# At most three of the first 26 bulk loads outstanding at a time, in an attention and rational-MLP kernel on one core

## The chip, the cores and the metric

The kernel runs on one NeuronCore of a Trainium2 chip. The metric is the device time of one execution in microseconds. Before the change three runs gave a median of 906.75 us (906.69 to 906.97).

## The reference, cut to what matters

```python
# q, k, v: (8 batches, 8 heads, 576 positions, 64)
scores = np.matmul(q, k.transpose(0, 1, 3, 2)) / sqrt(64)
# heads 0-3 see the last 32 positions; heads 4-7 every fourth of the last 128
scores = np.where(masks, scores, -1e9)
attn = exp(scores - max); attn = attn / (attn.sum(-1) + 1e-09)
x = (attn @ v)                          # as 4608 tokens x 512
h = x @ w_in                            # 512 -> 2048
P = a0 + a1*h + a2*h**2 + a3*h**3
Q = 1 + |b0|*|h| + |b1|*h**2
out = (P / (Q + 1e-6)) @ w_out          # 2048 -> 512
```

All inputs of the attention are float32; the two weight matrices come as 64-bit floats.

## The kernel before, in words

**Work.** The attention is cut into 48 units, six per batch. A unit loads one block of queries and keys (`load_qk`, 448 KB) and one of values (`load_v`, 384 KB). TensorE makes 48 small matmuls of scores, VectorE takes maxima and differences, ScalarE the exponentials, VectorE the sums and reciprocals, GpSimd the normalisation. In batch 0 TensorE then transposes the probabilities (three matmuls, `transposes`), somebody copies them out of the PSUM, and 48 more matmuls with the values (`av`) follow; VectorE transposes the result into place (`turn_out`). The MLP runs in tiles of 512 tokens x 128 hidden features, 144 of them: h matmuls, a rational function in about a dozen VectorE, ScalarE and GpSimd instructions, and out matmuls. All large matmuls split their operands into a high and a low part, except the first eight tiles, which use plain float32.

**Weights.** The 16 blocks of w_in and the 16 of w_out are loaded once (`w_fetch`, 512 KB each, since they are 64 bits wide). Each is turned into float32 by a scale on ScalarE (L718, tile wi_f or wo_f), a conversion of the low word on ScalarE or GpSimd (L318 or L726, tile wi_raw or wo_raw) and a join on VectorE (L324, tile w), and then split (tiles wi and wo).

**Order.** A planner (`Plan.run`) decides once, at build time, the order of the instructions of every engine, and each engine's queue is fixed in that order (`pin`). All transfers are issued by SyncE (SP), one after the other, by `load`; an SP instruction that waits holds up all SP instructions behind it. The tile framework has eight landing semaphores that transfers take in turn, so that a transfer is issued no earlier than the landing of the eighth one ahead of it, whatever its kind.

**The first transfers.** SP issues the six coefficients and the mask and then, in this order, the loads that are counted below as load 1 to 26 (q for a block of queries and keys, v for values, i for w_in, o for w_out): q q v q v q v q v q v q v i q v v o i o i, here two small stores of leftover tokens (left), o i q, another such store, o q. More small stores, the moves of batch 1's probabilities through HBM (turned, pT) and the other weights follow. Loads 1 to 11 and 13 are those of batch 0; the first h tile of the MLP needs all six units of batch 0 and load 14.

The instructions of the program itself come to the engines by DMA too; the profile counts them apart from the kernel's queue q1, as queues q8 and q14.

Of the kernel before, what the change touches and what calls it, by code (L numbers as in the profile page):

```python
# [19 lines left out]
P = 128  # L20
# [21 lines left out]

DEPTH, LOADS, STAGE, AHEAD, ON_PE = 2, 2, 6, 6, 2
PE_TURNS = 1
LEFT = S - 512
RQ, RKEY, NV = 4 * 3 * 32, 4 * 128, 3 * 2 * 2 * 64
LOG_SHIFT = 40
# [122 lines left out]
class Plan:  # L170
# [12 lines left out]
    def op(self, engs, rank, fn, *deps, dma=0, lock=False):  # L183
        o = Op(engs, rank, fn, deps, dma, lock)
        self.ops.append(o)
        return o
# [100 lines left out]
def tile_attention_moe(  # L287
# [10 lines left out]
    nc = tc.nc  # L298
# [8 lines left out]
    pin = tc.keep_in_program_order  # L307
# [3 lines left out]
    def load(dst, src):  # L311
        pin(nc.sync.dma_start(dst, src))

    def mm(o, lhs, rhs, start=True, stop=True):
        pin(nc.tensor.matmul(o, lhs, rhs, start=start, stop=stop))  # L315

# [43 lines left out]
    class Unit:  # L360
        def __init__(self, b, u):
            self.b, self.u, self.n = b, u, b * NU + u
            self.start, self.on_pe, self.pe_turn = b == 0, b < ON_PE, b < PE_TURNS
            self.s_tag, self.o_tag = (START_S[u], START_O[u]) if self.start else ("att", "att")
            self.s, self.o_ps = two_banks(self.s_tag), two_banks(self.o_tag)

        def load_qk(self, pool, tag):
            t = pool.tile([P, RQ + RKEY], F32, tag=tag, name=f"qk{self.n}", bufs=LOADS if pool is att else 1)
            load(t, qk[self.n])
            self.q = t[:, :RQ].rearrange("p (g i c) -> p g i c", g=4, i=3)  # L370
            self.k = t[:, RQ:].rearrange("p (g k) -> p g k", g=4)

        def load_v(self, pool, tag):
            self.v = pool.tile([P, NV], F32, tag=tag, name=f"v{self.n}", bufs=LOADS if pool is att else 1)
            load(self.v, vp[self.n])

        def scores(self):
            on_pe = self.on_pe
            if on_pe:

                for j, cnt, m in self.masks():
                    for r in range(j // 3, (j + cnt) // 3):
                        mm(self.s[:, r, :192], ident_b, m[:, 3 * r - j : 3 * r - j + 3], start=True, stop=False)
            for i in range(3):
                for g in range(4):
                    for r in range(2):
                        half = slice(64 * r, 64 * r + 64)
                        mm(self.s[32 * g : 32 * g + 32, r, 64 * i : 64 * i + 64], self.q[half, g, i], self.k[half, g, 32 * i : 32 * i + 64], start=not on_pe, stop=not on_pe or i == 2)
# [98 lines left out]
        def av(self):  # L487
            v_t = self.v.rearrange("p (i h e d) -> p i h e d", i=3, h=2, e=2)
            for i in range(3):
                for g in range(4):  # L490
                    h, e = g // 2, g % 2
                    for r in range(2):
                        half = slice(64 * r, 64 * r + 64)
                        c0, c1 = 192 + 64 * i, P * i + 32 * g if self.pe_turn else 96 * g + 32 * i
                        mm(self.o_ps[32 * g : 32 * g + 32, r, c0 : c0 + 64], self.pT[half, c1 : c1 + 32], v_t[half, i, h, e])
# [12 lines left out]
        def pieces(self):  # L508
# [14 lines left out]
            for s0, t0, step, num in segs:  # L523
                n_main = max(0, min(num, -(-(512 - t0) // step)))
                if num > n_main:

                    t1 = t0 + step * n_main - 512
                    to = LEFT * self.b + (t1 if step == 1 else LEFT // 4 * (t1 % 4) + t1 // 4)
                    left.append(((s0 + n_main, num - n_main), (slice(None), kts, slice(to, to + num - n_main))))
# [99 lines left out]
        def finish(self, av):  # L629
# [38 lines left out]
            if left:  # L668
                lf = op({"SP": 430 * len(left)}, self.by + 20.0, lambda e: self.put_left(), to, dma=P * 2 * LEFT * 4 + 60000)
                lf.count = len(left)  # L670
# [35 lines left out]
    def w_fetch(key):  # L706
        kind, n = key
        raw[key] = r = wpool.tile([P, 512], w_in.dtype, tag="%s%d" % key, name="%s_raw%d" % key)
        load(r, w_in[n] if kind == "wi" else w_out[n * P : (n + 1) * P, :])

    def w_words(key):
        return raw[key].bitcast(I32).rearrange("p (n two) -> p n two", two=2)
# [40 lines left out]

    def plan_weights(key):
        f = op({"SP": 430}, 0, lambda e: w_fetch(key), dma=512 * (8 if wide else 4) * P)
        early.append(f)
        if len(joined) >= AHEAD:
# [305 lines left out]
    for kt in range(NK):  # L1063
        r = NF * (NC - 2) + 2.0 + 2 * kt
# [99 lines left out]
```

## Time and profile before

| | |
|---|---|
| median of three runs | 906.75 us |
| profiled execution | 904.86 us |
| its span, first to last instruction | 903.1 us |
| mean granted TensorE clock | 0.992 of 2.4 GHz |
| PE busy | 879.2 us, 97% of the span, 8042 matmuls |
| DVE, ACT, POOL busy | 721.2, 669.4, 476.1 us |
| DMA | 89.24 MB, mean 99 GB/s |
| PE's share of the chain that ended last | 85% |

PE is TensorE, PEld its weight loads, DVE VectorE, ACT ScalarE, POOL GpSimd, SPq the instructions by which SyncE issues transfers. The profiled execution is 1.76 us longer than its span; the runs shown have a median 1.89 us above the profiled execution. Times in the rows count from the span's start.

### The profile page before, as it was taken

What the parts mean: (1) busy time and instruction counts of PE and PEld (TensorE: products, weight loads), DVE (VectorE), ACT (ScalarE), POOL (GpSimd) and SP (SyncE); (2) the same over time, 40 slices, a digit from 0 to 9 for tenths busy, and PEclk for the clock granted to TensorE, in tenths of its full rate; (3) what the DMA queues carried; (4) which work ended last, traced back from release to release, by engine and by line L of the source; (5) the groups of instructions that cost most, each with busy time, mean ns of one, the idle gap of its engine ahead of it and who ended that gap; (6) DMA issues with size and microseconds to landing.
All of it is one profiled execution on the core that took longest, in us unless ns stands there. A gap on an engine that the chain in (4) does not pass through costs nothing.

```text
span 903.1 us, 20437 instructions
## 1 busy us (share of the span) xinstructions
PE 879.2 (97%) x8042; PEld 689.5 (76%) x8042; DVE 721.2 (80%) x1301; ACT 669.4 (74%) x1070; POOL 476.1 (53%) x434
## 2 busy tenths in 40 slices
PE   5699999999999999999999999999999999999998
PEld 3344588888888888888888888888888888888886
DVE  4899999998998788887877888866986677656655
ACT  1977798877667778777777777777777777777766
POOL 1767366754545565654555555554555444444433
PEclk9899999999999999999999999999999999999999
DMA  9955851421523234332312335311420020001001
GB/s 342 318 181 156 296 184 42 141 76 67 180 84 107 65 109 160 112 94 68 131 48 77 90 114 153 92 35 32 143 58 18 1 82 0 1 1 48 1 0 47
DMA packets 70880, 89.24 MB, mean 99 GB/s; under 512 B 37376, under 2 KB 48256, under 8 KB 70784
## 3 DMA queue, kind: packets, MB, share of 16 engines
q1 hardware_dynamic: 70784, 87.94, 30.0%
q8 instruction: 63, 1.03, 0.5%
q14 instruction: 33, 0.27, 0.1%
HBM read 68.13 MB, written 19.79 MB: 97 GB/s over the span
## 4 chain that ended last, share of the span: by engine, by line
PE 85%; DVE 8%; ACT 2%; issue 2%; POOL 2%; DMA 0%; SPq 0%; DVEq 0%; POOLq 0%; ACTq 0%
PE out L315 40%; PE h L315 39%; PE pair L315 5%; DVE h L324 1%; DVE a L324 1%; DVE w L324 1%; ACT r L318 1%; DVE t L321 1%; DMA qk<-in_qk_dram 0%; POOL a L327 0%; DVE sm L442 0%; POOL p L327 0%; PE pair_A L315 0%; DVE wo L321 0%; DVE y L506 0%
## 5 line engine op out<-in xcount | busy, mean ns | idle before, releaser
L315 PE MATMUL h<-xh,wi 128*128 128x512 f32 x1072 | 356.7, 394 | 0.6 <-DVE a L324 0.6
L315 PE MATMUL out<-gh,wo 128*128 128x512 f32 x1072 | 332.1, 391 | 0.0
L327 POOL TENSOR_TENSOR a<-r,a 128x512 f32<-128x512 f32 x127 | 164.2, 1293 | 296.6 <-ACT r L318 285.3
L315 PEld LDWEIGHTS h<-xh,wi 128*128 128x128 f32 x1072 | 201.1, 188 | 48.4 <-DVE a L324 3.9
L315 PEld LDWEIGHTS out<-gh,wo 128*128 128x128 f32 x1072 | 200.0, 188 | 42.2
L315 PE MATMUL out<-gl,wo 128*128 128x512 f32 x536 | 209.0, 390 | 0.7 <-POOL gl L327 0.7
L315 PE MATMUL h<-xl,wi 128*128 128x512 f32 x536 | 208.8, 390 | 0.0
L324 DVE SCALAR_TENSOR_TENSOR a<-a,r 128x512 f32<-128x512 f32 x141 | 103.6, 735 | 105.6 <-ACT r L318 102.5
L327 POOL TENSOR_TENSOR gl<-a,gh 128x512 fp32r<-128x512 f32 x123 | 161.8, 1316 | 11.5 <-ACT gh L318 10.9
L318 ACT ACTIVATE r<-a,ln_bias 128x512 f32<-128x512 f32 x141 | 101.7, 721 | 89.1 <-POOL a L327 83.2
L318 ACT ACTIVATE t<-h,na_t 128x512 f32<-128x512 f32 x142 | 109.7, 772 | 28.9 <-PE h L315 28.3
L318 ACT ACTIVATE r<-a,ab_t 128x512 f32<-128x512 f32 x141 | 115.0, 816 | 20.9 <-DVE h L324 13.2
L324 DVE SCALAR_TENSOR_TENSOR h<-h,na_t,r 128x512 f32<-128x512 f32 x142 | 106.7, 751 | 14.4 <-ACT r L318 13.9
L315 PEld LDWEIGHTS out<-gl,wo 128*128 128x128 f32 x536 | 100.6, 188 | 22.8 <-POOL gl L327 1.8
L315 PEld LDWEIGHTS h<-xl,wi 128*128 128x128 f32 x536 | 100.7, 188 | 20.4 <-POOL xl L327 0.2
L324 DVE SCALAR_TENSOR_TENSOR h<-t,na_t,h 128x512 f32<-128x512 f32 x142 | 106.8, 752 | 4.1
L318 ACT ACTIVATE r<-r,exp_bias 128x512 f32<-128x512 f32 x144 | 104.0, 723 | 4.4
L321 DVE TENSOR_TENSOR t<-t,h 128x512 f32<-128x512 f32 x142 | 96.2, 678 | 9.8 <-ACT t L318 8.4
L318 ACT ACTIVATE a<-h 128x512 f32<-128x512 f32 x140 | 82.6, 590 | 27.1 <-PE h L315 26.6
L324 DVE SCALAR_TENSOR_TENSOR a<-a,h 128x512 f32<-128x512 f32 x132 | 90.3, 684 | 3.8
L318 ACT ACTIVATE gh<-a 128x512 fp32r<-128x512 f32 x122 | 75.9, 622 | 11.8 <-DVE a L324 9.6
L327 POOL TENSOR_TENSOR p<-p,sm 128x384 f32<-128x384 f32 x48 | 40.9, 855 | 36.1 <-DVE sm L446 28.3
(123 smaller groups left out, 771.9 us busy)
## 6 DMA issues: line engine op xcount, KB each, us to landing
qk<-in_qk_dram SPq DMA_DIRECT2D x48, 448.0 KB, 4.7
v<-in_vp_dram SPq DMA_DIRECT2D x48, 384.0 KB, 3.7
out_dram<-os SPq DMA_DIRECT2D x36, 256.0 KB, 2.3
wi_raw<-in_w_in_dram SPq DMA_DIRECT2D x16, 512.0 KB, 6.7
wo_raw<-in_w_out_dram SPq DMA_DIRECT2D x16, 512.0 KB, 6.4
turned<-u SPq DMA_DIRECT2D x42, 192.0 KB, 2.0
pT<-turned SPq DMA_DIRECT2D x84, 96.0 KB, 2.6
part<-os SPq DMA_DIRECT2D x4, 256.0 KB, 5.8
```

Source lines behind the costliest of these rows:

```text
L315: pin(nc.tensor.matmul(o, lhs, rhs, start=start, stop=stop))
L318: pin(nc.scalar.activation(o, i, func, **kw))
L321: pin(nc.vector.tensor_tensor(o, x, y, op))
L324: pin(nc.vector.scalar_tensor_tensor(o, x, s, y, op0, op1))
L327: pin(nc.gpsimd.tensor_tensor(o, x, y, op))
```

## The change: what it does

A second helper, `load_bulk`, does what `load` does, and counts its transfers in a list. For those with numbers 3 to 25 of the list (the fourth to the twenty-sixth) it adds a dependency on the transfer three places earlier in the list: SP waits until that one has landed. The blocks of queries and keys, of values and of weights are loaded by it; the coefficients, the mask, the stores and the moves through HBM still go by `load` and aren't counted. The order of all instructions on all engines is the same.

```diff
+BULK, GATED = 3, 26
...
+    bulk = []
+
+    def load_bulk(dst, src):
+
+        d = nc.sync.dma_start(dst, src)
+        pin(d)
+        if BULK <= len(bulk) < GATED:
+            tc.add_manual_dep(d.ins, bulk[-BULK].name, mybir.DependencyInfo(mybir.DependencyClass.Sync, mybir.DependencyReason.DATA), reason="few transfers at once")
+        bulk.append(d.ins)
+
...
-            load(t, qk[self.n])
+            load_bulk(t, qk[self.n])
...
-            load(self.v, vp[self.n])
+            load_bulk(self.v, vp[self.n])
...
-        load(r, w_in[n] if kind == "wi" else w_out[n * P : (n + 1) * P, :])
+        load_bulk(r, w_in[n] if kind == "wi" else w_out[n * P : (n + 1) * P, :])
```

## Rows read from the trace of the kernel before

**Rows 1.** The page: busy time of PE, and the span in 40 slices of 22.6 us (PE's busy tenths, the granted clock in tenths).

```profile
PE 879.2 (97%) x8042; PEld 689.5 (76%) x8042; DVE 721.2 (80%) x1301; ACT 669.4 (74%) x1070; POOL 476.1 (53%) x434
...
PE   5699999999999999999999999999999999999998
...
PEclk9899999999999999999999999999999999999999
```

**Rows 2.** Waits of PE in the first 60 us: who waited for whom, us in total, times, longest.

```profile
PE out L315 <- DVE g L324: 4.7, 1, 4.7
PE pair_B L315 <- issue: 3.2, 1, 3.2
```

**Rows 3.** The chain of waits in order of time, 16.5 to 28.5 us: start us, us, what.

```profile
16.57 3.18 issue
19.75 0.38 PE pair_B L315 x2
...
22.71 0.92 PE t L455 x3
...
25.64 1.13 PE pair_A L315 x48
...
27.45 0.98 DVE w L324
```

**Rows 4.** The timeline of DVE at the same place: start us, us, instruction, and in brackets the idle time before it and who ended that.

```profile
16.95 0.16 DVE L419 TENSOR_SCALAR mx<-mx 128x6 f32<-128x6 f32 x1
20.15 0.65 DVE L506 STREAM_TRANSPOSE x<-pair_B 128x192 f32<-128x192 f32 x2 [3.04 <-PE pair_B L315]
```

**Rows 5.** First the page's line for the queue q8 over the whole span, and the same queue from the start to 17.2 us, to 17.3 us and to 213.6 us (queue, kind: packets that have started, MB, share), and all packets of the stretch from 213.4 to 213.6 us; then the stretches from the start to 12.50, 17.27 and 213.51 us (start:end length, busy us and count in brackets of PE, PEld, DVE, ACT and POOL, granted clock, DMA share, GB/s).

```profile
q8 instruction: 63, 1.03, 0.5%
...
q8 instruction: 1, 0.02, 0.4%
...
q8 instruction: 2, 0.03, 0.8%
...
q8 instruction: 18, 0.29, 0.5%
...
DMA packets 1, 0.02 MB, mean 82 GB/s; under 512 B 0, under 2 KB 0, under 8 KB 0
...
0.00:12.50 12.50, 5.82 (x190) 3.94 (x192) 5.06 (x14) 2.53 (x4) 2.85 (x13) 1.00 0.82 286
...
0.00:17.27 17.27, 9.76 (x350) 6.93 (x351) 8.55 (x23) 4.07 (x7) 3.49 (x14) 1.00 0.87 320
...
0.00:213.51 213.51, 194.26 (x2246) 131.84 (x2247) 191.02 (x361) 159.47 (x270) 125.94 (x130) 0.97 0.55 189
```

**Rows 6.** SP's timeline: start us, us, transfer. These are loads 11, 14, 15, 19, 21, 22, 23, 24, 25 and 26, and the two small stores that come after load 26.

```profile
7.94 0.33 SPq L312 DMA_DIRECT2D v<-in_vp_dram  x1
...
11.38 0.33 SPq L312 DMA_DIRECT2D wi_raw<-in_w_in_dram  x1
13.49 0.33 SPq L312 DMA_DIRECT2D qk<-in_qk_dram  x1
...
17.70 0.33 SPq L312 DMA_DIRECT2D wi_raw<-in_w_in_dram  x1
...
19.74 0.33 SPq L312 DMA_DIRECT2D wi_raw<-in_w_in_dram  x1
...
27.90 1.17 SPq L312 DMA_DIRECT2D wo_raw<-in_w_out_dram  x1
29.12 0.42 SPq L312 DMA_DIRECT2D wi_raw<-in_w_in_dram  x1
29.64 0.38 SPq L312 DMA_DIRECT2D qk<-in_qk_dram  x1
...
30.66 0.49 SPq L312 DMA_DIRECT2D wo_raw<-in_w_out_dram  x1
31.97 0.33 SPq L312 DMA_DIRECT2D qk<-in_qk_dram  x1
...
34.26 1.03 SPq L312 DMA_DIRECT2D left<-y  x2
```

**Rows 7.** DMA issues of one transfer each (KB, us from issue to landing): load 1, issued at 1.65 us; load 19, issued at 17.70; a block of queries and keys issued at 82.4 us and one of values issued at 173.7 us, each with no other transfer ahead of it.

```profile
qk<-in_qk_dram SPq DMA_DIRECT2D x1, 448.0 KB, 4.0
...
wi_raw<-in_w_in_dram SPq DMA_DIRECT2D x1, 512.0 KB, 9.0
...
qk<-in_qk_dram SPq DMA_DIRECT2D x1, 448.0 KB, 3.5
...
v<-in_vp_dram SPq DMA_DIRECT2D x1, 384.0 KB, 2.9
```

**Rows 8.** The timeline of ACT where loads 18 and 19 are first read: start us, us, instruction.

```profile
28.12 0.73 ACT L318 ACTIVATE wo_raw<-wo_raw,low_bias 128x512 int32<-128x512 uint32 x1
...
29.32 0.74 ACT L318 ACTIVATE wi_raw<-wi_raw,low_bias 128x512 int32<-128x512 uint32 x1
```

**Rows 9.** Three stretches, with the columns of Rows 5: the one with the clock at half, the one after the longest wait of PE, and the rest of the span from 75 us on.

```profile
19.00:29.20 10.20, 7.48 (x226) 5.25 (x227) 7.52 (x21) 5.85 (x20) 3.68 (x5) 0.50 0.88 339
...
46.30:49.70 3.40, 3.40 (x6) 1.11 (x4) 3.40 (x4) 3.37 (x6) 1.66 (x2) 0.50 0.86 293
...
75.00:903.00 828.00, 822.49 (x7047) 659.33 (x7036) 662.64 (x1183) 621.21 (x980) 433.46 (x382) 1.00 0.26 83
```

## The prediction

> **What bounds the kernel now.** I read the page first, for where PE is idle, then PE's waits, the chain in order of time, and the timelines around the first transfers. PE is busy for 879 of 903 us and idle only in the first slices [rows 1]; from 75 us on it is busy 822.5 of 828 us [rows 9]. So a microsecond is won or lost in the start alone, and counts in full if the chain of the start is that much earlier where the dense stretch begins.
>
> Two waits of PE in the start are long. The 4.7 us for VectorE's g belong to the MLP's first tile. The other, 3.2 us, has no releaser: "issue", the engine waited for nothing that the profile shows [rows 2]. The chain passes through it: 3.18 us from 16.57 on, in the midst of a run of equal matmuls, and then VectorE, which has been idle for 3.04 us, goes on with the transpose of what these matmuls made [rows 3, 4]. After it the chain is PE, VectorE, ScalarE and GpSimd work.
>
> What PE waited for shows in the queue q8. Its 63 packets of 1.03 MB stand against PE's 16084 recorded instructions, 255 to a packet of 64-byte instructions: they are PE's program [rows 1, 5]. The second packet starts between 17.2 and 17.3 us, within the idle 3.18 us, when 701 instructions have started [rows 5]; PE goes on 2.48 us after 17.27. Far on, with no other transfer under way, the eighteenth packet starts when 4493 have started, 115 short of 18 x 256 [rows 5]. By the same measure the second was due at 512 - 115 = 397, and PE had begun 382 at 12.50 [rows 5], so it was due at about 12.6 us and came 4.7 us late. All that time the loads filled the DMA engines (share 0.82 up to 12.50 and 0.87 up to 17.27, at 286 and 320 GB/s, the empty first microseconds included) [rows 5]. I read it as an instruction packet that stood behind the loads' descriptors.
>
> The loads themselves: eight are outstanding at a time, since each issue waits for the landing of the eighth one ahead. Load 11 is issued at 7.94 when load 3 lands, load 21 at 19.74 when load 13 does. The ten steps between take 11.80 us, 1.18 each; one, 11.38 to 13.49, is 2.11, just after the first packet; without its extra 1.03 a load takes 1.08 us [rows 6].
>
> **The change part by part.** *The instruction packet.* From the due time of 12.6 to the stall at 16.57 lie 4.0 us, and a packet needs 2.48 from its start to PE: a delay of up to 1.5 us costs nothing, each microsecond more one of PE's. With three loads outstanding at most 3 x 1.08 = 3.2 us of loads can stand ahead: stall 1.7, so 3.04 - 1.7 = 1.3 us won on VectorE's wait [rows 4]. At the other end none stands ahead, and all 3.04 go. If the lateness has another cause, nothing goes. I take the middle of the queue, 1.6 us: 0.1 us of stall is left, and the chain is 2.9 us earlier.
>
> The Trainium skill says otherwise (DMA: Bandwidth & Descriptors, Queues, rings and completion order): each DMA engine goes round-robin between the queues for which it has work, a packet at a time. By that rule an instruction packet waits for a load's packet or so however many loads are queued, and the change would win nothing; that result is the first rival. The 4.7 us of delay speak against it, unless the packet was also asked for late.
>
> *The gates' own cost.* Each gated load is issued when the third one ahead has landed, so three loads take at least as long as one alone from issue to landing. Alone a block of values takes 2.9 us, one of queries and keys 3.5; load 1, in the cold start, took 4.0 [rows 7]. Three steps take 3 x 1.08 = 3.2 us. So the gates cost from nothing (2.9) over 0.1 us a load (3.5) to 0.26 a load (4.0); a gain is not excluded either, since the first loads then share the engines with fewer, but they land one after the other already, and I give it nothing. Nearest are the lone transfers. Only the queries' loads exceed 3.2, by 0.3; up to load 19 five triples end on such a load, but a late landing is partly made up by the next one, which has its data queued: I take a third of 5 x 0.3, 0.4 to 0.5 us later at load 19, with 0 and 16 x 0.26 = 4.2 us as ends.
>
> *What that delay meets.* Load 19 lands at 17.70 + 9.0 = 26.7 us [rows 6, 7] and ScalarE reads it at 29.32, after load 18 at 28.12 [rows 8]: 2.6 us of room. If the chain is 2.9 us earlier, ScalarE wants it at 26.4, and it lands at 27.1 or 27.2: ScalarE waits 0.7. ScalarE is close to full in that stretch and feeds the first h and out tiles, so I count it: 2.9 - 0.7 = 2.2 us won.
>
> *What is queued behind the gates on SP.* Up to load 21 nothing but loads. Load 22 was issued at 27.90, after stores that waited for VectorE, and now also waits for load 19 (26.7): no cost. Loads 23 and 24 wait for 20 and 21, which follow load 19 by some 1.25 us each (27.9 and 29.2); they were issued at 29.12 and 29.64: none. Load 25 waits for load 22, which alone takes 3.5 to 4.0 from 27.90, so 31.4 to 31.9 against 30.66, and load 26 for load 23, a step on, about 33 against 31.97 [rows 6, 7]. Behind it the next stores stood at 34.26 [rows 6]: a microsecond of room, cost nothing. If all work comes 2.2 us earlier, those stores want 32.1 and these gates cost SP a microsecond; the stores and load 27 are read much later, so I leave it at nothing. The other 22 loads and the moves are not gated, and the waits themselves are SP's, which is idle.
>
> *Sum.* -2.9 + 0.7 = -2.2 us. Against the profiled execution (span 903.1, 904.9 with what lies around it) that is 902.7; the runs' median is 1.9 above it, 906.75, and becomes 904.6. The likeliest case alone spans a gain of 1.2 to 3.0: 903.7 to 905.6.
>
> **The rivals.** *Nothing is won.* The packet is late for another reason, or three loads keep the engines as full as eight, and the stall stays. For it: 4.7 us of delay is some four loads and not eight, so the queue ahead of the packet may be bounded by something shorter than the outstanding loads, and three would come near that bound. Against it: three steps are still less than 4.7 us. Also in it: the dependency orders nothing that the queue didn't. Time 906.7, give or take 0.5.
>
> *Slower: the loads become the bound.* Load 19 has 29.32 - 26.7 = 2.6 us of room over the 16 loads since load 3, so from 2.6 / 16 = 0.16 us more per load (1.24, a triple of 3.7 us) ScalarE waits for weights, whether or not PE's stall is gone. At the 4.0 us of load 1 it is 0.26 per load, load 19 lands 4.2 us later and ScalarE waits 1.6: 908.4. For it: load 1's time, and that three outstanding leave no reserve if one of the 16 engines lags, as after the first packet (the step of 2.11). Against it: both lone transfers lie under 3.7.
>
> *More is won, by the clock.* The granted clock is 0.50, the 1.2 GHz level, from 19.0 to 29.2 us, after PE's idle 3.18; and again from 46.3, after the 4.7 [rows 2, 9]. Three pieces of the chain lie in the first stretch, 0.38 + 0.92 + 1.13 = 2.43 us [rows 3]. If PE stays busy and the clock stays up, half of that is won too: 904.6 - 1.2 = 903.4. Against it: PE is busy only 7.5 of those 10.2 us [rows 9] with waits for VectorE and GpSimd that stay.
>
> **How the numbers follow.** Forecast 0.46, nothing won 0.28, slower 0.15, clock 0.11. A measurement here tells 0.2% from no change, 1.8 us, so faster is below 904.9 and slower above 908.6 for my chances. Of the forecast's 0.46 some 0.38 lies below 904.9; with the clock and a little chance, faster 0.50. Slower: the case's time of 908.4 lies at the edge, and with delays up to several us more half to two thirds of it are beyond; with some unnamed mishap 0.14. The rest, 0.36, is the same. The range takes in the gain of the clock and most of the slower case: 903.0 to 907.8.
>
> **What would show it.** Right: in the profile after, PE's wait on "issue" near 16.6 us is gone or under 1 us, the second q8 packet starts before 16 us, VectorE's transpose starts near 17 us, and PE's dense stretch begins about 2 us earlier. The loads' issues follow each other by 1.1 us as before. Wrong: the packet still starts near 17 us (nothing won); or issues follow each other by 1.25 us or more, and ScalarE or PE waits for DMA of wi_raw, wo_raw or qk (slower). It would also be wrong if the start is shorter and the dense stretch begins when it did, because something in 30 to 75 us, such as the SP queue or the later weights, does not move with it.

## The result, and the profile after

The change makes the kernel slower: 912.4 us (median of 6 runs, 909.7 to 915.0) where the kernel before has 906.9 in the same comparison, a ratio of 1.0057 with an interval of 1.0033 to 1.0081. The forecast was 904.6 us and the range ended at 907.8. The profiled execution took 913.5 us, with a span of 911.7, 8.6 us more than the profiled one before; the medians lie 5.6 apart.

The page after, busy times, the 40 slices of PE, clock and DMA, and the chain by engine:

```profile
PE 882.0 (97%) x8042; PEld 691.0 (76%) x8042; DVE 720.6 (79%) x1301; ACT 669.6 (73%) x1070; POOL 475.7 (52%) x434
...
PE   5779999999999999999999999999999999999998
...
PEclk9699999999999999999999999999999999999999
DMA  7973771313433234331221334310521020001001
...
PE 84%; DMA 7%; DVE 6%; ACT 2%; issue 1%; POOL 1%; SPq 0%; POOLq 0%; ACTq 0%; DVEq 0%
```

PE's work is the same [rows 1]; its idle time and the clock's low stretches are in the first slices again. New is that 7% of the chain is DMA, where it was 0%. SP's timeline after, cut to loads 6, 7, 10, 12, 13, 16 with 17, and 21 (start us, us, transfer):

```profile
7.81 0.33 SPq L319 DMA_DIRECT2D qk<-in_qk_dram  x1
9.71 0.33 SPq L319 DMA_DIRECT2D v<-in_vp_dram  x1
...
14.10 0.33 SPq L319 DMA_DIRECT2D qk<-in_qk_dram  x1
...
16.86 0.33 SPq L319 DMA_DIRECT2D qk<-in_qk_dram  x1
20.00 0.33 SPq L319 DMA_DIRECT2D v<-in_vp_dram  x1
...
23.30 2.37 SPq L319 DMA_DIRECT2D v<-in_vp_dram  x2
...
31.50 0.33 SPq L319 DMA_DIRECT2D wi_raw<-in_w_in_dram  x1
```

A load is now issued when the third one ahead has landed, so load 3 landed at 7.8 us and load 13 at 23.3: ten steps of 1.55 us, where they were 1.18 [rows 6]. Load 21 is issued at 31.5 instead of 19.7 and lands at 36.3 instead of 29.2. Who waited, in the first 60 us: first PE, then ScalarE (ACT), then GpSimd (POOL) (us in total, times, longest).

```profile
PE h L326 <- ACT x L329: 4.6, 1, 4.6
...
PE pair L326 <- DMA pT<-turned: 2.0, 1, 2.0
PE pair_B L326 <- issue: 1.9, 1, 1.9
```

```profile
ACT wo_raw L329 <- DMA wo_raw<-in_w_out_dram: 4.6, 2, 3.6
```

```profile
POOL wo_raw L737 <- DMA wo_raw<-in_w_out_dram: 4.0, 1, 4.0
```

The wait on "issue" is there, at 1.9 us instead of 3.2 [rows 2]. But ScalarE and GpSimd now wait for weights: ScalarE reads load 18 at 31.51 instead of 28.12 us [rows 8].

```profile
31.51 0.76 ACT L329 ACTIVATE wo_raw<-wo_raw,low_bias 128x512 int32<-128x512 uint32 x1 [3.59 <-DMA wo_raw<-in_w_out_dram]
```

PE's second h tile waits 4.6 us for ScalarE behind them and starts at 38.49 instead of 35.31 us (PE's timeline, before and after):

```profile
35.31 5.64 PE L315 MATMUL h<-x,w 128*128 128x512 f32 x12 [0.94 <-ACT x L318]
```

```profile
38.49 8.27 PE L326 MATMUL h<-x,w 128*128 128x512 f32 x12 [4.57 <-ACT x L329]
```

The loss then grows, to 6.6 us at PE's matmul of 57.76 us (64.36 after). The chain shows a part of how (start us, us, what):

```profile
41.82 4.20 DMA turned<-u
46.02 0.02 issue
46.04 7.90 DMA pT<-turned
53.94 0.14 issue
54.08 2.37 PE pair L326 x97
```

Loads 27 to 30, which no gate holds, were issued at 42.3 to 45.2 us, just ahead of the moves of batch 1's probabilities. They were issued ahead of them before, too, at 35.84 to 39.95 us, but spread wider. A move that had taken 5.95 us took 7.9 behind them, and PE waited 2.0 us for it.

### The profile page after: what moved, and what is told of

Read it like the earlier page. It is cut to its first block, busy times and chain, and to the rows that moved or that the text cites. A ratio compares the mean times of both kernels' runs of the same rounds, so it can differ in the third digit from the quotient of the medians.

```text
span 911.7 us, 20435 instructions
## 1 busy us (share of the span) xinstructions
PE 882.0 (97%) x8042; PEld 691.0 (76%) x8042; DVE 720.6 (79%) x1301; ACT 669.6 (73%) x1070; POOL 475.7 (52%) x434
## 3 DMA queue, kind: packets, MB, share of 16 engines
q8 instruction: 63, 1.03, 0.5%
## 4 chain that ended last, share of the span: by engine, by line
PE 84%; DMA 7%; DVE 6%; ACT 2%; issue 1%; POOL 1%; SPq 0%; POOLq 0%; ACTq 0%; DVEq 0%
PE out L326 40%; PE h L326 39%; PE pair L326 5%; DMA qk<-in_qk_dram 2%; DMA v<-in_vp_dram 1%; DMA left<-y 1%; DVE h L335 1%; DMA pT<-turned 1%; DVE w L335 1%; DVE a L335 1%; DMA turned<-u 1%; DVE t L332 1%; DMA wi_raw<-in_w_in_dram 1%; DMA wo_raw<-in_w_out_dram 0%; ACT r L329 0%
## 5 line engine op out<-in xcount | busy, mean ns | idle before, releaser
L329 ACT ACTIVATE a<-h 128x512 f32<-128x512 f32 x140 | 82.6, 590 | 26.7 <-PE h L326 26.1
L329 ACT ACTIVATE gh<-a 128x512 fp32r<-128x512 f32 x122 | 75.9, 622 | 11.8 <-DVE a L335 9.7
L338 POOL TENSOR_TENSOR p<-p,sm 128x384 f32<-128x384 f32 x48 | 40.9, 854 | 35.4 <-DVE sm L457 30.9
```

Source lines behind the costliest of these rows:

```text
L329: pin(nc.scalar.activation(o, i, func, **kw))
L338: pin(nc.gpsimd.tensor_tensor(o, x, y, op))
```

## The experiments

In each, the kernel before ran beside on the same chip; ratios are against that. "Step" is the time between the landings of loads 3 and 13, divided by ten. Where a run stands below with a time alone, it was executed once.

**How many loads outstanding.** One number of the change is altered.

```diff
-BULK, GATED = 3, 26
+BULK, GATED = 4, 26      # e1; 5 in e2, 2 in e3, 1 in e13
```

Four:

> At most four loads outstanding instead of three. Theory A (queues run dry: a load takes some 4.7 us from issue to landing even with few ahead, so the step between landings is 4.7 us divided by the number outstanding): step 1.2 us instead of the change's 1.58, load 21 lands near 29 to 30 us instead of 36.3, time 906 to 908. Theory B (each gate costs its own half microsecond on SP whatever the depth): step 1.5 or more, load 21 near 35 us, time 911 to 912. Theory C (the loads' landings do not matter, the loss comes from the moves and stores that stand behind the gates on SP): time falls by a quarter of the loss at most, 910 to 912, since the gates are still there.

Five:

> At most five outstanding. Theory A: 4.7 / 5 = 0.94 us, below the 1.08 us that the engines need, so the step is that of before, load 21 lands near 29 us, and the second instruction packet still stands behind less than before: PE's idle on issue near 17 us falls under the 3.2 us of before; time 905 to 907, no slower than before. Theory B: still 910 to 912.

Two:

> At most two outstanding (the second load is not gated, the third to the twenty-sixth are). Theory A: 4 to 4.5 us divided by two, a step of 2.0 to 2.2 us, load 21 lands near 46 us, ten later than with three; time 919 to 924. Theory B: the same step as with three, 1.58 us, time 912 to 913. The second instruction packet: if it stands behind the loads, it starts before 15 us and PE's idle on issue is under 1 us.

One:

> One load outstanding at a time. The prediction took 3.2 us from issue to landing for a load alone (2.9 and 3.5 far on in the kernel). If that holds in the start too, the step is 3.0 to 3.5 us, load 13 lands near 5 + 12 x 3.2 = 43 us, and what failed is that two loads ahead add 1.4 us to it. If a load alone takes 4 us or more here (the cold start's 4.0), the step is 4 us or more and the lone transfers were the wrong rows.

| outstanding | step, us | step x number: issue to landing | GB/s, 12 to 24 us | second packet, us after PE's 397th instruction | PE's idle on issue near 17 us | ratio to before |
|---|---|---|---|---|---|---|
| 8 (before) | 1.18 | 9.4 | 410 | 4.7 | 3.18 | 1 |
| 5 | 1.13 | 5.6 | 377 | 3.1 | 1.26 | 0.9996 (0.9987 to 1.0006) |
| 4 | 1.34 | 5.4 | 326 | 2.0 | 1.54 | 0.9996 (0.9987 to 1.0006) |
| 3 (the change) | 1.55 | 4.7 | 257 | 2.3 | 1.88 | 1.0057 (1.0033 to 1.0081) |
| 2 | 1.89 | 3.8 | 231 | 2.1 | 0.19 | 1.0169 (1.0153 to 1.0185) |
| 1 | 3.16 | 3.2 | 143 | 2.1 | none | 951.6 us in one run beside 905.1 |

PE's 397th recorded instruction, weight loads counted, is where the prediction put the moment at which the second packet is due.

The stretch from 12 to 24 us in the kernel before, with five, four, three, two and one (length, busy us and count of PE, PEld, DVE, ACT, POOL, granted clock, DMA share, GB/s):

```profile
12.00:24.00 12.00, 8.26 (x288) 5.93 (x288) 7.35 (x21) 2.35 (x6) 1.73 (x3) 0.79 1.03 410
```

```profile
12.00:24.00 12.00, 8.01 (x347) 5.93 (x326) 8.98 (x28) 4.99 (x18) 2.57 (x4) 0.92 1.01 377
```

```profile
12.00:24.00 12.00, 7.57 (x350) 5.71 (x349) 9.49 (x29) 4.46 (x17) 2.90 (x5) 1.00 0.94 326
```

```profile
12.00:24.00 12.00, 8.34 (x302) 6.04 (x301) 8.01 (x22) 3.00 (x11) 1.77 (x3) 0.85 0.81 257
```

```profile
12.00:24.00 12.00, 8.01 (x257) 6.01 (x256) 6.69 (x19) 1.54 (x3) 1.66 (x3) 1.00 0.73 231
```

```profile
12.00:24.00 12.00, 4.89 (x154) 3.69 (x154) 3.64 (x10) 0.99 (x2) 1.06 (x2) 1.00 0.46 143
```

The DMA engines run dry: the two last columns fall with every load fewer. Theory B, a fixed cost per gate, falls with the row of four. Theory A has the sign right, and its constant of 4.7 us wrong: with four the step was to be 1.2 us and load 21 to land near 30, and they came at 1.34 and 32.6; with five load 21 lands at 31.2, 2 us later than before, at no cost in time. One load alone takes 3.2 us in the start too, as the lone rows said [rows 7]; what they didn't say is that each load outstanding beside it adds 0.6 to 0.9 us (3.2, 3.8, 4.7, 5.4), while the engines are busy for only 0.46, 0.73, 0.81 and 0.94 of the time. So three take 4.7 us, not 3.2.

The stall is a less steady quantity than one column suggests. A second trace with five outstanding (e11 below) has PE idle for 3.52 us and the packet 4.4 us after the 397th instruction, although up to load 14 its loads are those of e2; one with eight (e9) has 2.32 and 3.7, one with four (e10) 1.90 and 2.8, one with three up to load 13 (e4) 0.70 and 1.9. So the packet comes sooner with four and fewer (1.9 to 2.8 us) than with five and eight (3.1 to 4.7), but five and eight can't be told apart; with six halves of loads (e12 and e14 below) it came after 2.2 and 3.7. Some 2.1 us are left even with one load outstanding, so not all of the 4.7 us was the loads' doing. With two the packet starts at 17.41 us, not before 15, because PE itself waited for its loads.

With four, the first part of the forecast is there: PE's timeline (start us, us, instruction, idle before it and who ended it).

```profile
17.30 0.27 PE L326 MATMUL pair_B<-v,pT 64*32 64x64 f32 x2 [1.54 <-issue]
...
35.44 1.22 PE L326 MATMUL h<-x,w 128*128 128x512 f32 x1 [3.79 <-ACT x L329]
```

PE goes on at 17.30 instead of 19.75 [rows 3], and up to the first h tile all its work is 2.4 to 3 us earlier (29.66 against 32.39). The second h tile starts at 35.44 instead of 35.31: ScalarE had to wait for weights that landed 3.0 to 3.4 us later than before (load 21 at 32.6). What the instruction packet gave, the weights took.

**Which loads are gated.** With three outstanding, only the first part, and only the second:

```diff
-BULK, GATED = 3, 26
+BULK, GATED = 3, 13                                # e4
...
-        if BULK <= len(bulk) < GATED:
+        if 13 <= len(bulk) < GATED:                # e5
```

> Three outstanding for loads 4 to 13 only (the attention's first loads); loads 14 to 26 are free. Theory A: load 13 lands near 23 us as with the change, the weights then land 1.1 to 1.3 us apart, load 21 near 32 to 33 us instead of 36.3; ScalarE wants them from 29 us on: about half of the loss is left, time 908 to 910. Theory C (what stands behind the gates of loads 22 to 26 on SP makes the loss): time as before, 906.9. If the attention's own loads make the loss by PE's waits for them (0.3 to 1.2 us each): 910 to 912.

> Three outstanding for loads 14 to 26 only; loads 4 to 13 are free as before. Queues run dry: load 13 lands near 20 us as before, then steps of 1.5 to 1.6 us, load 21 near 32 to 33 us; PE's idle on issue near 16.6 us stays 2.5 to 3.2; ScalarE or GpSimd waits for the weights; with the late weights on top of the late PE the time is 908 to 911. If the loss came from the attention's loads alone, it is the time of before, within 0.2%.

Gates on loads 4 to 13 alone cost 0.20% (1.0010 to 1.0029 around 1.0020; load 13 lands at 23.3, load 21 at 33.1), on 14 to 26 alone 0.18% (1.0008 to 1.0028; load 13 at 20.0, load 21 at 32.7). The first is within what was expected, the second at its lower edge. Each costs some 1.7 us; together they cost 5. Load 21 is 3.9 and 3.5 us late in the two, and 7.1 late with both: the late landings add up, and the 2.6 us of room that the prediction found before ScalarE's read can be used only once. That last step is argued from the sums. That stores and moves behind the gates make the whole loss (theory C) does not hold: e4 has no gate after load 13 and pays.

**Only the first loads, five outstanding.**

```diff
-BULK, GATED = 3, 26
+BULK, GATED = 5, 13
```

> Five outstanding for loads 4 to 13, then free. If the instruction packet stands behind the loads and five are enough to keep the engines full: load 13 lands near 19.7 us, load 19 near 27, PE's idle on issue 1.3 us or less, the chain 2 us earlier at 20 us; the weights land when they did, so of the 2 us at most 1.5 are kept: 904.0 to 905.5 where the kernel before has 905.5. If the weights' landing (DMA throughput up to load 21) is the real bound of the first h tile: no gain, 905.3 to 906.

The landings are those of before (load 13 at 19.8, 19 at 26.7, 21 at 29.2), so here the gates cost the loads nothing, and still there is no gain: 1.0008 (0.9999 to 1.0016). Its PE timeline, and the same transposes in the kernel before:

```profile
18.41 0.27 PE L326 MATMUL pair_B<-v,pT 64*32 64x64 f32 x2 [2.97 <-issue]
...
30.17 0.87 PE L466 MATMUL t<-ident,p 128*128 128x128 f32 x3 [1.68 <-issue]
```

```profile
30.03 0.52 PE L455 MATMUL t<-ident,p 128*128 128x128 f32 x3 [0.25 <-PE pair_B L315]
```

PE reaches the first stall 1.1 us sooner and leaves it 1.3 us sooner (18.41 against 19.75); the stall itself, which was to be 1.3 us or less, stays at 2.97. Near 28.5 us it runs out of instructions again, for 1.68 us, and goes on at 30.17, where before it went on at 30.03. The fourth packet starts at 27.6 us in both kernels, when the freed loads 18 to 21 fill the queue. In the kernel before PE goes on with the same transposes 2.4 us after that packet starts, as after other packets; its gap there is only 0.25 us, and the profile names PE itself as the releaser, so that the packet would have been next there too is read from these times.

**Other orders.** If late weights eat the gain, weights issued earlier should keep it: loads 15 to 17, which batch 1 needs, are held until load 21 is issued, with no gates, with four and with five outstanding.

```diff
...
-            o.fn(eng)
+            if o.bulk:
+                seen += 1
+            if o.bulk and seen in (15, 16, 17):
+                held.append((o.fn, eng))
+            else:
+                o.fn(eng)
+            if o.bulk and seen == 21:
+                for fn, e in held:
+                    fn(e)
...
```

> No load gated, as before, but loads 15, 16 and 17 (batch 1) issued after loads 18 to 21 (weights): these weights land some 3 us earlier, near 23 to 26 us. If PE's late instruction packets and not the weights set the first h tile in the kernel before: no gain over before (905.0 to 906.0), PE's idle on issue near 17 us stays about 3 us. If the weights set it: 903 to 904.5.

> The same order, with at most four outstanding of the first 26. With four in the old order the chain was 3 us earlier at 21 us and lost that to weights that landed 2 to 3 us later. If those two are the whole story, the earlier weights keep most of it: first h tile near 30 us, the second near 33, time 903 to 904.5. If something else in the start takes the gain (the fourth instruction packet, the moves on SP): 905 to 906.

> The same order, with at most five outstanding. With five in the old order the fourth instruction packet came at 28.0 us and held PE to 30.5. If the packet stands behind five loads again: PE on issue near 29 us, time 905 to 906. If not: like four, 903 to 904.5.

None is faster: 1.0006 (0.9997 to 1.0015), 1.0008 (1.0000 to 1.0017) and 1.0009 (0.9998 to 1.0020). With four, PE's timeline shows where it stays (columns as above):

```profile
17.57 0.37 PE L334 MATMUL pair_B<-v,pT 64*32 64x64 f32 x2 [1.90 <-issue]
...
29.21 0.87 PE L474 MATMUL t<-ident,p 128*128 128x128 f32 x3 [1.48 <-issue]
```

Both the second and the fourth packet hold PE up, 1.90 and 1.48 us, and the second h tile follows the first without a wait: the weights are no longer what is late. With five the two stalls are 3.52 and 1.59 us. So with the weights out of the way PE stands at the instruction packets again, and no version here beats the kernel before.

**What makes a load slow beside others.** First fewer instruction packets, with the change's gates (e7) and without (e8), by leaving out two thirds of batch 0's score matmuls:

```diff
...
-            for i in range(3):
+            for i in range(1 if self.start else 3):
...
```

> The change, with 16 instead of 48 score matmuls in each of the six units of batch 0 (32 of 48 score blocks of that batch are left out, the mask alone stands in their place): 384 recorded PE instructions less, so about three instruction packets instead of five before load 21 lands. If every packet that holds up one of the 16 engines delays a landing and with it the next issue (1 to 2 us each): load 21 lands 2 to 4 us earlier than with the change, at 32 to 34 us. If only the time from issue to landing counts: 35.5 to 37 us.

> The kernel before (no load gated), with the same 32 of 48 score blocks of batch 0 left out. Both theories: with eight outstanding a packet is absorbed but for the first, so load 21 lands where it did, 28 to 29.5 us. PE's idle on issue is gone or moved; if the first h tile starts no earlier than 31 us although PE has a third of that work less, the weights' landing and the VectorE and ScalarE work bound the start.

With the gates, load 21 lands at 35.9 us against 36.3, what the second theory expected; but four packets started before it and not three, so this is weak. Up to load 13, with two packets started instead of three, it was 1.8 us earlier (21.5); from there to load 21, with two more in both, it took 1.4 us longer. The time was 908.6 us. Without gates load 21 lands at 28.8, the time was 903.1 us, and PE's first stall is gone, but a later packet, which starts at 28.95, now holds PE for 2.32 us (until 31.34).

Then the same bytes outstanding in smaller pieces, by partitions (e12) and by columns (e14):

```diff
-BULK, GATED = 3, 26
+BULK, GATED = 6, 52
...
+        for half in (slice(0, 64), slice(64, 128)):       # e12; column halves in e14
+            half_bulk(dst[half], src[half])
...
```

> The change with each load cut into two transfers of 64 partitions, at most six halves outstanding: the same bytes outstanding as with three loads, refilled in smaller pieces. If the bytes outstanding alone set the step: 1.5 to 1.6 us per load, load 21 near 36 us, 911 to 913. If what counts is that a refill is held until the last of the 16 engines has finished a whole load, so that the others run dry: 1.2 to 1.4 us per load, load 21 at 30 to 33 us, 907 to 909.

> Each load cut into two of half the columns (128 partitions each), at most six halves outstanding. Halves of 64 partitions moved at 238 GB/s with the engines busy, so that they told nothing about gates. If halves of 128 partitions move at the full rate: with the bytes outstanding as the cause 1.5 to 1.6 us per load, load 21 near 36 us; with the wait for the last engine of a whole load as the cause 1.2 to 1.4 us, load 21 at 30 to 33 us.

Halves of 64 partitions missed both expectations: 1.92 us per load, load 21 at 45.1, a ratio of 1.032. The reason isn't the gates, since the engines were busy all the time and moved little:

```profile
12.00:24.00 12.00, 8.38 (x277) 5.80 (x264) 6.41 (x18) 1.53 (x3) 1.66 (x2) 1.00 1.04 237
```

Halves by columns end where whole loads do, load 21 at 36.1 us, 913.1 us in one run: the size of the pieces alone makes no difference. SP's timeline shows how they got there:

```profile
15.85 0.97 SPq L325 DMA_DIRECT2D qk<-in_qk_dram  x2
19.64 0.86 SPq L325 DMA_DIRECT2D v<-in_vp_dram  x2
```

Between 11.8 us and this point the halves landed 0.5 to 0.65 us apart, 1.0 to 1.3 us per load, as was expected if the wait for a whole load's last engine were the cause; and then nothing was issued for 2.8 us, because the next landing came 3.2 us after the one before it, around the second instruction packet (which starts at 17.2). After the change load 10 does the same, 3.1 us after load 9 (issues of 16.86 and 20.00). The kernel before has one step of 2.1 and no other over 1.3 [rows 6].

What held the issue there is in the trace too: a load's landing is recorded as sixteen counts, and a gate opens with the last. In e14 fifteen counts of the half in question are in at 17.30 us and the last at 19.63. With the change fifteen counts of load 10 are in at 18.25 and the last at 19.98; loads 11 and 12 lag in the same way (1.7 and 1.6 us), load 13 no longer (0.2). So halves don't escape the wait for the last count, and e14 does not rule it out. In the kernel before one count of load 7 falls 1.2 us behind the other fifteen, just after the first packet, and one does so in each load up to load 12: the lag is carried on and not caught up. From load 7 to load 21 the first and the last count are always 2.0 to 2.1 us apart, so that it costs the one long step. From the issue, half of the counts are in after 2.8 us and the last after 3.2 with one load outstanding, after 3.6 and 4.7 with three, 7.3 and 8.7 with eight (means of loads 4 to 21).

## Why the prediction was wrong

- *What bounds the start.* Right in the main: of the 8.6 us between the two profiled executions 6.6 are lost by 64 us; of the rest, 1.4 us are more idle time of PE between 100 and 300 us (2.0 instead of 0.6). That the second packet stands behind the loads holds in part: it comes 3.1 to 4.7 us after PE's 397th instruction with eight and five loads outstanding and 1.9 to 2.8 with four and fewer. By the Trainium skill (DMA: Bandwidth & Descriptors, Queues, rings and completion order) each DMA engine takes turns between the queues, a packet at a time. By that rule the number of loads queued would change nothing; these runs disagree, and the measurement decides. Whether it is the number that counts, or that the engines are full with five and eight (busy share 1.01 and 1.03) and not with four and fewer, they don't tell.
- *The instruction packet.* Right in sign, too large: 0.1 us of stall was to be left, and 1.9 were. The packet started 2.3 us after the 397th instruction and not 1.6, it took 2.0 us instead of 1.1, and PE went on 3.3 us after its start and not 2.5. That 4.7 us of delay were all the queue's was too much: 2.1 stay with a single load outstanding.
- *The gates' own cost.* This is the step that failed: "Nearest are the lone transfers". A load alone does take 3.2 us (e13), but three at a time take 4.7, so a load costs not 0.1 us more but 0.4 to 0.5, beyond even the upper end of 0.26. It was the size of a term: load 19 was to land at 27.1, at worst 30.9, and landed at 33.4 us. Ten steps of 1.55 us are also the sign that the prediction itself had named for being wrong in this way, 1.25 us or more.
- *What that delay meets.* The mechanism was right, ScalarE and GpSimd waiting for weights. This is the rival "slower", given a chance of 0.15, with its sign and its place. Its point, 1.24 us per load, lies between the step of 1.13 with five, where ScalarE waits 0.5 us for load 18, and 1.34 with four, where it waits 2.3 and gain and loss cancel. Its price of 1.6 us was too low by the same term.
- *What is queued behind the gates on SP.* Costed at nothing; PE waited 2.0 us there. Loads 27 to 30 were issued within 3 us ahead of the moves (pT), and PE waited for a move. The prediction looked at when SP is free and not at what it then issues all at once.
- *The sum.* Even without any cost of the gates the gain would not have come: e6 has the landings of before and gains nothing, since its first stall hardly shrinks and the fourth instruction packet is late next; e10 has the weights in time, and the same packet takes most of its gain (PE is 2.2 us ahead of the kernel before at 17.57 us and 0.8 at 29.21), which leaves too little to show in the time. The prediction named the weights as next and took no row on the later packets.
- *The clock.* With the change the clock is at 0.50 from 20.4 to 30.6 us again; the rival that lives on it didn't occur. It is at 0.50, the 1.2 GHz level, twice more, around and after the new waits (37.4 to 44.3 and 54.5 to 57.9 us), where it was once before (46.3 to 49.7 [rows 9]). The second h tile's matmuls took 8.27 us instead of 5.64 by that, and most of it came back in a shorter wait for g behind them (2.5 us instead of 4.7).

What stays open: why a load takes longer beside others while the engines still run dry. Of the 1.4 us that two loads beside it add, 0.8 stand in the middle count and 0.6 in the lag of the last behind it. Loads 4 to 21 take 28.5 us with the change and 21.3 before; of the 7.2 us between them single long steps near the five instruction packets make a part (3.1 instead of 1.1 at load 10). That the packets make a count late is read from the times in three traces; e7 left out only one of them, and how much of the whole they cause was not separated.

## What to carry to other kernels

Time a transfer in the company in which it will run: from a lone transfer's 3.2 us one would have said that three outstanding keep the engines full, and it took five (busy share 1.01, and still 377 GB/s instead of 410). A gate that waits for a whole load waits for the last of its sixteen counts. Before shortening a DMA queue for the sake of something small behind it, count what the large transfers lose, and look for the next small thing that comes late: here the second instruction packet came earlier and the weights, then the fourth packet, took its place. Read a stall of 1 to 3 us from more than one trace: with five loads outstanding it was 1.26 us in one and 3.52 in another.

## What the runs showed of the hardware

- Transfers of 64 partitions moved at 237 GB/s with a DMA share of 1.04, those of 128 partitions at 410 with 1.03: halves of queries and values by partitions landed 0.8 to 1.0 us apart there, whole loads 0.9 to 1.2 in the kernel before.
- PE's instructions come in packets of 16 KB that take about 1 us each, and where PE had run out it went on 2.2 to 2.7 us after such a packet started, 3.3 where the packet itself took 2.0 (with the change). PE's waits on issue that the profiles name all end within the first 32 us, where the loads are under way.
- With the change the executions differ more from each other, 909.7 to 915.0 us, than those of the kernel before, 905.6 to 908.3.
